# x + gamma * y on one core: from three row blocks with small lead loads to one block of 128 rows per partition, in fewer and larger transfers

## The chip, the core and the metric

The kernel runs on one core of one Trainium2 chip. The metric is device time in microseconds (us) of one execution. The core has compute engines that work side by side (here TensorE, called PE, and VectorE, called DVE, do the arithmetic), queues that only issue transfers in this kernel (SyncE, called SP, and ScalarE, called ACT), and 16 DMA engines that move data between HBM and the on-chip memory SBUF, which has 128 partitions.

## The reference

```python
B, S, D = 1024, 16, 512
x: bf16 (B, S, D)    y: bf16 (B, S, D)    gamma: bf16 (D)

def reference(x, y, gamma):
    return x + gamma * y
```

Seen as rows, x, y and the output are 16384 rows of 512 bf16 numbers, 1 KB a row. So 128 rows belong to each of the 128 partitions. x and y are 16.78 MB each and are read once; the output of 16.78 MB is written once: 50.33 MB in all, with very little arithmetic for it.

## The kernel before

**Layout.** The 16384 rows are cut into three blocks in HBM (`BLOCKS`, line 7): 4, 64 and 60 rows per partition. Inside a block, each partition owns consecutive rows, so partition p of the 64-row block starts 64 KB after partition p-1, and of the 60-row block 60 KB after it (`rows_of`). All of y stays in SBUF (`y_sb`, 128 rows per partition); x has a smaller buffer (`x_sb`, 76 rows), whose rows are used twice. The result is written over y in `y_sb` and stored from there.

**Transfers.** Two lists written out by hand give the order of the transfers. Below, y(4,68) means rows 4 to 67 of every partition. `SP` (lines 12 to 19) issues y(0,4), y(4,68), x(4,68), y(68,128), x(68,120), x(120,128). `ACT` (line 20) issues x(0,4), gamma, and the stores s(4,68), s(0,4), s(68,128). One issue cuts the transfer into one packet for each partition, as long as the partition's part (64 rows are 65536 bytes), so each of the 16 DMA engines gets 8 packets, and a 4-byte packet that signals a semaphore at the end. Each of the two issuing queues is worked off in the order of its issues.

**What holds an issue back.** The function `ring` (line 96) writes out both lists. `EARLY = (2, 1)` (line 22): the first two SP transfers and the first ACT transfer are put into the block of instructions that stands ahead of the start barriers of all engines. `HOLD` and `AHEAD` (line 24): the third transfer of SP and the second of ACT wait until PE has seen y(0,4) land (lines 149 to 151); DVE learns of that landing in the same way. x(68,120) is written into rows 24 to 75 of `x_sb`, so its issue waits for the add of piece 2; x(120,128) goes into rows 0 to 7 and waits for the add of piece 0. `RELEASE` (line 26): when x(68,120) has landed, PE lets ACT issue the stores (`s_go`, line 158) and lets DVE use the piece (`s_rel`, line 159). So no store is issued until nearly everything is loaded. A store also waits for the adds of the pieces that it holds.

**Arithmetic.** PE copies gamma to all partitions by a matmul with a row of ones (line 152), and DVE casts it to bf16 in SBUF (line 154). Then DVE works through its own list (line 28) over five pieces of 8, 16, 44, 52 and 8 rows: multiplications m0, m1, m2 (line 180), additions a2, a0, a1 (line 189), then m3, m4, a3, a4. Each is one instruction over a whole piece, in place in `y_sb`.

Of the kernel before, what the change touches and what calls it, by code (L numbers as in the profile page):

```python
# [3 lines left out]

BLOCKS = [4, 64, 60]

PIECES = [8, 16, 44, 52, 8]


SP = [
    ('y', 0, 4),
    ('y', 4, 68),
    ('x', 4, 68, 4),
    ('y', 68, 128),
    ('x', 68, 120, 24),
    ('x', 120, 128, 0),
]
ACT = [('x', 0, 4, 0), ('g',), ('s', 4, 68), ('s', 0, 4), ('s', 68, 128)]  # L20

EARLY = (2, 1)

HOLD, AHEAD = ('y', 0, 4), (2, 1)

RELEASE = ('x', 68, 120, 24)

DVE = [('m', 0), ('m', 1), ('m', 2), ('a', 2), ('a', 0), ('a', 1), ('m', 3), ('m', 4), ('a', 3), ('a', 4)]
MULT, ADD = mybir.AluOpType.mult, mybir.AluOpType.add
# [2 lines left out]
def _take(sem, n, eng):  # L32


    return eng.wait_ge(sem, n).then_inc(sem, -n)  # L35


def kernel(
# [9 lines left out]
    nc = tc.nc  # L48
# [8 lines left out]
    rows = N // P  # L57
    n = len(PIECES)
    assert sum(PIECES) == rows
    starts = [sum(PIECES[:c]) for c in range(n + 1)]  # L60
    dt = xf.dtype
    edges = [sum(BLOCKS[:c]) for c in range(len(BLOCKS) + 1)]
    assert edges[-1] == rows

    def rows_of(t, a, b):

        c = max(c for c in range(len(BLOCKS)) if edges[c] <= a)
        assert b <= edges[c + 1]
# [6 lines left out]
    y_sb = nc.alloc_sbuf_tensor("y_sb", [P, rows, D], dt).ap()  # L75
    x_loads = [w for w in ACT + SP if w[0] == "x"]
    y_loads = [w for w in SP + ACT if w[0] == "y"]
    stores = [w for w in SP + ACT if w[0] == "s"]
    for loads in (x_loads, y_loads, stores):
# [7 lines left out]
    s_load = {w: sem("s_" + "_".join(map(str, w[:2]))) for w in x_loads + y_loads}  # L87
    s_held = {nc.sync: sem("s_held_sp"), nc.scalar: sem("s_held_act"), nc.vector: sem("s_held_dve")}
# [4 lines left out]
    def meets(a, b, c, d):  # L93
        return a < d and c < b
# [4 lines left out]
    def x_at(row):  # L99
        return next(w[3] + row - w[1] for w in x_loads if w[1] <= row < w[2])  # L100
# [12 lines left out]
    def ring(eng, what, n_early, n_ahead):  # L113

        known, went = 0, False
        for k, w in enumerate(what):
            kind = w[0]
            if k == n_ahead:
                _take(s_held[eng], 1, eng)
            need = frees(w) if kind == "x" else pieces_of(w[1], w[2]) + list(w[3:]) if kind == "s" else []  # L120
            need = max((order[c] + 1 for c in need), default=0)
            if kind == "s" and not went:
                _take(s_go, 1, eng)
                went = True
            if need > known:
                eng.wait_ge(s_add, need)
                known = need
            if kind == "g":
                i = eng.dma_start(out=gamma_row, in_=gamma.unsqueeze(0)).then_inc(s_gamma, 16)
            elif kind == "x":  # L130
                to = x_sb[:, w[3] : w[3] + w[2] - w[1], :]
                i = eng.dma_start(out=to, in_=rows_of(xf, w[1], w[2])).then_inc(s_load[w], 16)
            elif kind == "y":
                r = slice(w[1], w[2])
                i = eng.dma_start(out=y_sb[:, r, :], in_=rows_of(yf, w[1], w[2])).then_inc(s_load[w], 16)
            else:
                r = slice(w[1], w[2])
                i = eng.dma_start(out=rows_of(of, w[1], w[2]), in_=y_sb[:, r, :]).then_inc(s_out, 16)
            if k < n_early:
                early.append(i.ins)  # L140

    ring(nc.sync, SP, EARLY[0], AHEAD[0])
    ring(nc.scalar, ACT, EARLY[1], AHEAD[1])


    nc.vector.memset(ones_row, 1.0).then_inc(s_ones, 1)  # L146
    _take(s_load[HOLD], 16, nc.tensor)
    for s_one in s_held.values():
        nc.tensor.sem_inc(s_one, 1)
    _take(s_ones, 1, nc.tensor)  # L150
    _take(s_gamma, 16, nc.tensor)
    nc.tensor.matmul(gamma_ps, ones_row, gamma_row, start=True, stop=True).then_inc(s_ps, 1)  # L152
# [3 lines left out]

    _take(s_load[RELEASE], 16, nc.tensor)
    nc.tensor.sem_inc(s_go, 1)
# [4 lines left out]
    def need(loads, c):  # L163
        for w in loads:
            if w not in landed and meets(starts[c], starts[c + 1], w[1], w[2]):
                if w == RELEASE:
                    _take(s_rel, 1, nc.vector)
                elif w == HOLD:
                    _take(s_held[nc.vector], 1, nc.vector)
                else:  # L170
                    _take(s_load[w], 16, nc.vector)
                landed.add(w)

    for kind, *args in DVE:
        c = args[0]
        yt = y_sb[:, starts[c] : starts[c + 1], :]
        if kind == "m":
            need(y_loads, c)
            g = gamma_sb[:, None, :].to_broadcast([P, PIECES[c], D])
            nc.vector.tensor_tensor(out=yt, in0=yt, in1=g, op=MULT).then_inc(s_dve, 1)  # L180
            open_mults += 1
        else:
# [4 lines left out]
            at = x_at(starts[c])  # L187
            xt = x_sb[:, at : at + PIECES[c], :]
            nc.vector.tensor_tensor(out=yt, in0=xt, in1=yt, op=ADD).then_inc(s_add, 1)  # L189
# [44 lines left out]
```

## Time and profile before

| | |
|---|---|
| median of 3 runs | 119.63 us (119.6 to 119.88) |
| span of the profiled execution, first to last instruction | 118.2 us |
| median less span (what lies around the span) | 1.4 us |
| DVE busy | 70.1 us, 59% of the span |
| PE busy | 0.6 us |
| bytes moved | 50.33 MB, 426 GB/s over the span |

The profile is one execution. Its times are in us from the span's start. It lists the compute instructions with their durations, the transfers with the moment of issue and of landing (a transfer has landed when its last semaphore signal arrives), and the DMA packets. For a window of time it gives the number of packets that start in it, their bytes, and their total time as a share of 16 engines over the window. So the mean time of one packet is share x 16 x window length / packets. A packet is counted with its full length in the window in which it starts, so a share over a short window can be over or under 100%.

The moments that the steps below use, from the timeline and the trace's landings (all us):

| transfer | issued | landed |
|---|---|---|
| y(0,4) | 0.00 | 3.38 |
| x(0,4) | 0.13 | 4.34 |
| y(4,68) | 0.42 | 23.81 |
| x(4,68) | 3.71 | 43.21 |
| gamma | 3.90 | 11.45 |
| y(68,128) | 4.09 | 61.34 |
| x(68,120) | 55.37 | 77.06 |
| x(120,128) | 57.58 | 79.53 |
| s(4,68) | 77.41 | 98.90 |
| s(0,4) | 77.81 | 100.12 |
| s(68,128) | 94.43 | 118.19 |

DVE's work: the memset of the ones 1.99, the cast of gamma 12.32, m0 to m2 from 23.95, a2, a0, a1 from 43.45, m3 and m4 from 61.80, a3 and a4 from 78.17 to 94.39.

### The profile page before, as it was taken

Reading aid. Unit: us, or ns where it says so; the run is one execution under the profiler, and the core shown is the slowest. Engines: PE = TensorE matmul, PEld = TensorE weight load, DVE = VectorE, ACT = ScalarE, POOL = GpSimd, SP = SyncE. Lnnn points to the kernel's source line nnn. Section 1 sums busy time; section 2 is a strip of 40 time slices with the busy share of each in tenths; the row PEclk is TensorE's granted clock in tenths of the full one; section 3 lists DMA queues with packets and bytes.
Section 4 is the critical chain, followed back from the end, with each engine's and each line's share of the span. In section 5 each row is a group of like instructions: output and inputs, shape, how many; then the busy total and the mean of one; then the engine's idle time right before and its main releaser. Section 6 shows DMA issues by size and latency. Waiting matters only on the chain. (4 is left out here: it accounts for less than half of the span.)

```text
span 118.2 us, 91 instructions
## 1 busy us (share of the span) xinstructions
PE 0.6 (0%) x1; PEld 0.1 (0%) x1; DVE 70.1 (59%) x12; POOL 0.2 (0%) x4
## 2 busy tenths in 40 slices
PE   0000100000000000000000000000000000000000
PEld 0000000000000000000000000000000000000000
DVE  0000200089999969999999999999999900000000
POOL 0000000000000000000000000000000000000000
DMA  6999889988899879879969696898899889799793
GB/s 248 461 666 399 355 355 399 665 355 355 355 599 466 355 333 624 374 333 499 499 288 576 288 576 288 360 637 355 355 576 488 355 355 510 333 582 416 333 499 166
DMA packets 1442, 50.33 MB, mean 426 GB/s; under 512 B 161, under 2 KB 162, under 8 KB 546
## 3 DMA queue, kind: packets, MB, share of 16 engines
q1 hardware_dynamic: 864, 33.03, 64.8%
q10 hardware_dynamic: 578, 17.30, 33.9%
HBM read 33.56 MB, written 16.78 MB: 426 GB/s over the span
## 5 line engine op out<-in xcount | busy, mean ns | idle before, releaser
L180 DVE TENSOR_TENSOR y_sb<-y_sb,gamma_sb 128x4096 bf16<-128x4096 bf16 (+3 forms) x5 | 34.7, 6981 | 10.9 <-DVEq L35 10.9
L189 DVE TENSOR_TENSOR y_sb<-x_sb,y_sb 128x4096 bf16<-128x4096 bf16 (+3 forms) x5 | 34.7, 6981 | 1.2 <-DVEq L35 1.1
L154 DVE CAST gamma_sb<-gamma_ps 128x512 bf16<-128x512 f32 x1 | 0.7, 692 | 10.2 <-DVEq L35 10.2
L146 DVE MEMSET ones_row<- 1x128 bf16 x1 | 0.2, 165 | 2.0 <-PEq L51 2.0
L152 PE MATMUL gamma_ps<-gamma_row,ones_row 1*128 1x512 bf16 x1 | 0.6, 581 | 11.6 <-PEq L35 11.6
L152 PEld LDWEIGHTS gamma_ps<-gamma_row,ones_row 1*128 1x128 bf16 x1 | 0.1, 101 | 11.6 <-issue 11.6
L218 POOL MEMSET const-bfloat16-1.0<- 128x1 bf16 x1 | 0.1, 101 | 0.0
L218 POOL MEMSET const-uint8-127<- 128x1 uint8 x1 | 0.1, 101 | 0.0
L218 POOL MEMSET const-float32-0.0<- 128x1 f32 x1 | 0.1, 98 | 0.2 <-issue 0.2
L218 POOL MEMSET const-float32-1.0<- 128x1 f32 x1 | 0.1, 98 | 0.0
## 6 DMA issues: line engine op xcount, KB each, us to landing
y_sb<-in_y_dram SPq DMA_DIRECT2D x1, 7680.0 KB, 57.3
out_dram<-y_sb ACTq DMA_DIRECT2D x1, 7680.0 KB, 23.8
x_sb<-in_x_dram SPq DMA_DIRECT2D x1, 6656.0 KB, 21.7
x_sb<-in_x_dram SPq DMA_DIRECT2D x1, 1024.0 KB, 22.0
y_sb<-in_y_dram SPq DMA_DIRECT2D x1, 512.0 KB, 3.4
x_sb<-in_x_dram ACTq DMA_DIRECT2D x1, 512.0 KB, 4.2
out_dram<-y_sb ACTq DMA_DIRECT2D x1, 512.0 KB, 22.3
y_sb<-in_y_dram SPq DMA_DIRECT2D x1, 23.4
```

The costliest lines, as they stand in the source:

```text
L146: nc.vector.memset(ones_row, 1.0).then_inc(s_ones, 1)
L152: nc.tensor.matmul(gamma_ps, ones_row, gamma_row, start=True, stop=True).then_inc(s_ps, 1)
L154: nc.vector.tensor_copy(out=gamma_sb, in_=gamma_ps).then_inc(s_dve, 1)
L180: nc.vector.tensor_tensor(out=yt, in0=yt, in1=g, op=MULT).then_inc(s_dve, 1)
L189: nc.vector.tensor_tensor(out=yt, in0=xt, in1=yt, op=ADD).then_inc(s_add, 1)
L218: nc = _bacc.Bacc("TRN2", target_bir_lowering=False, num_devices=1)
```

## The change

There is one block: partition p owns rows 128p to 128p+127, so its rows start 128 KB after those of partition p-1, in both loads and stores. y is loaded in two transfers of 64 rows, x in 64, 56 and 8, and the output is stored in two transfers of 64 rows. The pieces of DVE are 8, 12, 44, 56 and 8 rows, in the same order. Only y(0,64) stands ahead of the barriers. Nothing waits for a first landing any more: x(0,64), y(64,128) and gamma are issued as soon as the barriers are passed. x(64,120) goes into rows 20 to 75 of `x_sb` and waits for the add of piece 2 as before; x(120,128) goes into rows 0 to 7 and waits for the add of piece 0 as before. The stores wait for the landing of x(64,120).

```diff
-BLOCKS = [4, 64, 60]
+BLOCKS = [128]
-PIECES = [8, 16, 44, 52, 8]
+PIECES = [8, 12, 44, 56, 8]
 SP = [
-    ('y', 0, 4),
-    ('y', 4, 68),
-    ('x', 4, 68, 4),
-    ('y', 68, 128),
-    ('x', 68, 120, 24),
+    ('y', 0, 64),
+    ('x', 0, 64, 0),
+    ('y', 64, 128),
+    ('x', 64, 120, 20),
     ('x', 120, 128, 0),
 ]
-ACT = [('x', 0, 4, 0), ('g',), ('s', 4, 68), ('s', 0, 4), ('s', 68, 128)]
+ACT = [('g',), ('s', 0, 64), ('s', 64, 128)]
-EARLY = (2, 1)
+EARLY = (1, 0)
-HOLD, AHEAD = ('y', 0, 4), (2, 1)
+HOLD = None
+AHEAD = (None, None)
-RELEASE = ('x', 68, 120, 24)
+RELEASE = ('x', 64, 120, 20)
...
-    _take(s_load[HOLD], 16, nc.tensor)
-    for s_one in s_held.values():
-        nc.tensor.sem_inc(s_one, 1)
+    if HOLD:
+        _take(s_load[HOLD], 16, nc.tensor)
+        for s_one in s_held.values():
+            nc.tensor.sem_inc(s_one, 1)
```

## The prediction

> **What bounds the kernel now.** I read the DMA row of the 40 slices first, then the queues, then the chain of waits.
>
> ```profile
> span 118.2 us, 91 instructions
> ...
> DMA  6999889988899879879969696898899889799793
> ...
> q1 hardware_dynamic: 864, 33.03, 64.8%
> q10 hardware_dynamic: 578, 17.30, 33.9%
> ...
> issue 11%; DVE 3%
> ```
>
> The two queues' packets fill 64.8 + 33.9 = 98.7% of 16 engines' span, 116.7 us of 118.2. The trace's records of packets start at 1.00 and end at 117.85, so over the stretch in which there is anything to move the engines are full: the DMA engines are the bound, and DVE's 70.1 us are not. The low digits in the row are no gaps: a packet of 64 KB counts where it starts. The chain names little ("issue 11%") because it does not follow transfers. So the time is: 1.00 before the first packet, the packets of one DMA engine end to end, 0.36 until SP sees the last landing (117.85 to 118.21), and 1.4 around the span. The profiled span with 1.4 added is the median of the runs, 119.63; I make the sum against that.
>
> **What a packet costs.** Windows in which only one size starts give means (share x 16 x window / packets). In order: windows 82 to 97 (64 KB stores), 8 to 13 and 24 to 42 (64 KB loads), 101 to 117 (60 KB stores), 61 to 76 (52 KB loads), 98.6 to 99.2 (4 KB, its share includes rounding at the edges).
>
> ```profile
> q10 hardware_dynamic: 96, 6.29, 96.7%
> ```
> ```profile
> q1 hardware_dynamic: 32, 2.10, 97.1%
> ```
> ```profile
> q1 hardware_dynamic: 112, 7.34, 94.1%
> ```
> ```profile
> q10 hardware_dynamic: 112, 6.88, 99.2%
> ```
> ```profile
> q1 hardware_dynamic: 112, 5.96, 91.8%
> ```
> ```profile
> q10 hardware_dynamic: 63, 0.26, 104.3%
> ```
>
> This gives 0.967 x 16 x 15 / 96 = 2.418 us for a 64 KB store; for a 64 KB load 2.428 early and 2.420 later; 2.267 for 60 KB; 1.967 for 52 KB; 0.159 for 4 KB. The large ones all run at 27.1 bytes per ns. At that rate 4096 bytes would take 0.151, so each small packet wastes 0.008. No other operation of the kernel touches this sum.
>
> **Part by part, on one DMA engine** (8 packets for each transfer; group sums from the packet records, divided by 16 engines):
>
> - Removed: the three 4-row transfers, 24 packets of 4 KB. They took 1.36 (y) and 2.57 (x and store), 3.93 in all; at 0.159 they would be 3.82, so 0.11 is extra length of the very first packets.
> - Removed: 16 packets of 60 KB, 18.17 loaded and 18.14 stored, 36.31. Removed: 8 of 52 KB, 15.73.
> - Added: 16 packets of 64 KB, half loads, half stores: 16 x 2.419 = 38.70. Added: 8 packets of 56 KB. No row has this size; midway between 52 and 60 KB it is 2.117, bounds 1.967 and 2.267 for the price but hardly for the sum, as the bytes are fixed and the rate on both sides is 27.1; 8 x 2.117 = 16.93.
> - Removed: three transfers' semaphore packets on each engine, 9 ns each: 0.03.
>
> Sum: 38.70 + 16.93 - 3.93 - 36.31 - 15.73 - 0.03 = **-0.37**. If the 0.11 of the first packets returns on the first 64 KB ones, it is -0.26. The early 64 KB loads show that long packets get longer too (2.457 mean for the first 32, 2.428 for the next), so I keep most of it: **-0.28**.
>
> **The head.** y(0,4) is issued at 0.00 and its first packet starts at 1.00; y(0,64) is issued at the same place, as SP's first instruction. The other row for issue to first packet is the store of 64 KB packets, 77.41 to 78.73, 1.32, but on engines that were still busy with x(120,128). Ends: +0.32 (a long packet starts later) and -0.16 (the idle share between 1.0 and 2.0 goes, while the 16 engines start one after another). The nearest row is the load from SP with idle engines: 1.00, so nothing.
>
> **What the waits could spoil.** Each has cover, and I follow the landings to size it. The head is 8 rows shorter (2.54 in 4 KB packets, 2.65 with their extra), so y(0,64) lands near 21.2 and x(0,64) near 40.6. y(64,128) follows 8 x 2.42 later, 59.9; x(64,120) 76.8; x(120,128) 79.3; two stores of 19.34 each, 118.0.
>
> - The hold on y(0,4) goes: x(0,64), y(64,128) and gamma are issued near 2, not at 3.7 to 4.1. On SP nothing is gained, as y(0,64) fills the engines until about 20.4; this is also the cover, 18 us, for x(0,64) having to wait for the barriers. On ACT nothing stands ahead of gamma now but the barriers. It took 7.6 from issue to landing behind 64 KB packets; by that it lands before 11, PE and the cast add 1.6, and DVE first needs it at 21.2.
> - DVE: one row costs (14.02 - 11.89) / 8 = 0.267. m0 to m2 are 18.43 - 4 x 0.267 = 17.36, from 21.3 to 38.7; a2 starts at 40.8, and the three adds end at 58.1. m3 and m4 (16.22 + 4 x 0.267 = 17.29) start when y(64,128) lands, 60.0, and end at 77.3; a3 and a4 end at 94.9. DVE before was busy without a break from 43.45 to 94.39; now it has a rest of 1.9 before m3.
> - x(64,120) is issued at the end of a2, 52.8, x(120,128) at 55; the queue is not empty until 59.5. Cover 6.7 and 4.5; uncovered, each us late is a us.
> - The first store is let go at the landing of x(64,120), with x(120,128), 2.47 of packets, still to come: the same cover as before.
> - The last store is issued near 94.9, with 1.32 to its first packet 96.2; the first store keeps the engines busy until about 98.0. Before, it was 94.43 against 99.73. The cover falls from 4.0 to 1.8 but holds.
>
> So all of the change is -0.28: 119.63 - 0.28 = **119.35**. About 0.3% (0.36 us) is what a measurement of this kernel can tell from no change, so my likeliest case is "within 0.3%", on its fast side.
>
> **A rule against it.** Strided reading is in the trace: x(68,120) takes 52 of each 60 KB and its packets run at 27.08 bytes per ns, where stores without a stride reach 27.1. A pitch of 64 KB is there too, at 2.418. A pitch of 128 KB is not. The Trainium skill, "DMA: Bandwidth & Descriptors", section "Latency and other measured facts", says that copies between HBM tensors lose rate when the pitch from partition to partition in HBM is a large power of two: 207 GB/s at 512 KiB and 164 at 2 MiB, each way, against 214 when padded. It has no row for 128 KiB; if its loss at 512 KiB held here, an estimate from that page, the time would be about 3% longer, near 123. By the trace's rows, where 60 and 64 KB pitches run alike, the cost is nothing, and I go by those.
>
> **Rivals.**
>
> 1. *The start gets cheaper as well.* The first packets' extra (0.11 at 4 KB and 0.13 at 64 KB: 38.84 against 16 x 2.420 = 38.72) was due to small transfers from two queues meeting at 2.2 to 3.9, and the idle 0.16 goes. Then -0.37 - 0.13 = -0.50 to -0.66: 119.0 to 119.15. For it: the 64 KB loads of 3.65 start among the last packets of x(0,4). Against: packets that started at 13 to 18 are still long (97.4% x 16 x 5 / 32 = 2.435).
> 2. *A long first packet starts late*: +0.32 - 0.28, 119.67, no change.
> 3. *Slower: the 128 KB pitch.* 16 engines walk through HBM in step, 512 KB apart instead of 256 KB, and packets grow. Place: all 40 packets of 64 KB and 8 of 56 KB. Ends of the price: nothing, and what the worst row of 64 KB packets shows, the first 32 (2.457 against 2.418, +0.039): 48 x 0.039 = 1.87, so 119.35 + 1.87 = 121.2. It decides from (0.36 + 0.28) / 48 = 0.013 us per packet on. Against it: the same lengths at 60 and 64 KB pitch.
> 4. *DMA engines run dry before the last store*: only if DVE ends after 96.7, which would need 1.8 of new delay on it. I see none; small.
> 5. *It does not do what it says.* Were x(0,64) to go after the barriers only when y(0,64) has landed, the engines would stand still for about 1.5 near 20. No wait of that kind is in the SP list; negligible.
>
> **Numbers.** The case of 119.35, with 0.1 on both sides, has 0.5, and about a quarter of that lies beyond 0.3% faster. Rival 1 has 0.23, rival 2 has 0.09, rival 3 has 0.15, 4 and 5 have 0.03. Faster: 0.12 + 0.23 = 0.35. Slower: 0.15 + 0.03 = 0.18. Within: 0.47. The range is 118.95 to 119.95: it holds the likeliest case, rivals 1 and 2 with their bounds, and the mild part of rival 3.
>
> **What would show it.** Right: two queues' packets still fill the stretch from 1.0 to the end; 64 KB packets at 2.418 to 2.42 in windows of loads and of stores; 56 KB ones at 2.117; span near 117.9; last DVE add ending near 94.9, the last store's issue before the first one's packets end. Wrong: a first packet later than 1.3, 64 KB packets over 2.43 all along (rival 3), or a window late in the stores in which few packets run (rival 4). A span changed by more than 0.7 with packet lengths as before would mean that something outside the packet sum, which I take as fixed, has moved.

## The result, and the profile after

The changed kernel takes 120.05 us (median of 5, 119.88 to 120.24) against 119.65 of the kernel before, run beside it (119.6 to 119.88): ratio 1.0029, 95% interval [1.0018, 1.004]. It is slower by 0.3%, where 0.2% faster was forecast, and the time lies 0.1 us above the range that was forecast. The interval does not reach 1, so even less than the 0.3% that the prediction named can be told from no change.

The page of the changed kernel shows the same picture as before: the engines are full, in fewer packets.

```profile
span 118.6 us, 80 instructions
...
q1 hardware_dynamic: 720, 33.55, 66.1%
q10 hardware_dynamic: 290, 16.78, 32.7%
```

The two queues fill 98.8% of 16 engines' span, as they filled 98.7%, so there is still no gap to find. Either packets are longer than they should be, or the bytes are more, and the bytes are the same. So the length of the packets is read next, window by window: stores in 82 to 97, loads in 13 to 18, and then the second and the first packet of each engine (3.9 to 6.3, 1 to 2).

```profile
q10 hardware_dynamic: 96, 6.29, 96.7%
```
```profile
q1 hardware_dynamic: 32, 2.10, 96.7%
```
```profile
q1 hardware_dynamic: 16, 1.05, 100.8%
```
```profile
q1 hardware_dynamic: 16, 1.05, 311.8%
```

Stores take 0.967 x 16 x 15 / 96 = 2.418, loads 0.967 x 16 x 5 / 32 = 2.418, the second packet of each engine 1.008 x 2.4 = 2.419. But the first one takes 3.118 x 1 = **3.118 us**, 0.70 more. All 16 engines pay it side by side, once. The same window of the kernel before holds only 4 KB packets, which moved at 352 GB/s there (busy times of the engines, clock, DMA share, GB/s):

```profile
1.00:2.00 1.00, 0.00 (x0) 0.00 (x0) 0.01 (x1) 0.00 (x0) 1.00 0.94 352
```

DVE shows when the time was lost:

```profile
21.93 17.36 DVE L182 TENSOR_TENSOR y_sb<-y_sb,gamma_sb 128x4096 bf16<-128x4096 bf16 x3 [10.68 <-DVEq L36]
41.38 17.36 DVE L191 TENSOR_TENSOR y_sb<-x_sb,y_sb 128x22528 bf16<-128x22528 bf16 x3 [2.08 <-DVEq L36]
53.30 2.53 SPq L133 DMA_DIRECT2D x_sb<-in_x_dram  x2
60.62 17.29 DVE L182 TENSOR_TENSOR y_sb<-y_sb,gamma_sb 128x28672 bf16<-128x28672 bf16 x2 [1.88 <-DVEq L36]
77.80 17.96 ACTq L139 DMA_DIRECT2D out_dram<-y_sb  x2
78.09 17.30 DVE L191 TENSOR_TENSOR y_sb<-x_sb,y_sb 128x28672 bf16<-128x28672 bf16 x2 [0.18 <-DVEq L36]
```

The durations are those forecast (17.36 and 17.29), and every start is 0.5 to 0.65 late: 21.93 for 21.3, 41.38 for 40.8, 60.62 for 60.0. The shift is there at the first load and hardly grows. It happened before 21.

For each kernel I take the sum over its packets of what each lasts beyond the steady length of its size (2.418 for 64 KB, 2.267 for 60, 2.116 for 56, 1.966 for 52, 1.213 for 32, 0.607 for 16, 0.309 for 8, 0.159 for 4), divided by 16 engines. I call the part from packets that start in the first 5 us the **start loss**. The two profiled executions then differ like this:

| us, mean of 16 engines | before | changed | difference |
|---|---|---|---|
| start of the first packet | 1.12 | 1.14 | +0.02 |
| packets at steady length | 116.41 | 116.19 | -0.23 |
| start loss, and the same up to 20 us | 0.18, 0.25 | 0.70, 0.71 | +0.46 |
| extra length after 20 us | 0.06 | 0.12 | +0.06 |
| overlap of neighbouring records | -0.26 | -0.23 | +0.03 |
| mean end of the 16 engines | 117.59 | 117.93 | +0.35 |
| last engine behind the mean | 0.26 | 0.19 | -0.07 |
| last packet to end of span | 0.38 | 0.43 | +0.05 |
| span | 118.23 | 118.55 | +0.33 |

The gain in the packets came as forecast. In these two executions the start took twice as much; how much of that belongs to the kernels, the repeats r1 to r3 below show.

### The profile page after: what moved, and what is told of

Read it like the earlier page. It is cut to its first block, busy times and chain, and to the rows that moved or that the text cites. A ratio compares the mean times of both kernels' runs of the same rounds, so it can differ in the third digit from the quotient of the medians.

```text
span 118.6 us, 80 instructions
## 1 busy us (share of the span) xinstructions
PE 0.6 (0%) x1; PEld 0.1 (0%) x1; DVE 70.2 (59%) x12; POOL 0.2 (0%) x4
```

## The experiments

**Theory 1**: an engine that starts idle loses time once, and loses more when its first packet is long; small lead packets avoid part of it. **Rivals**: the pitch of 128 KB (theory 2); something the core does in the first microseconds, such as barriers and issues (theory 3). Later ones are named where they come up. The median of the kernel before moves between 119.65 and 119.81 with the chip, so kernels are compared by their ratio to the runs of it beside them.

**e1: a 4-row lead in the changed kernel.**

```diff
-    ('y', 0, 64),
+    ('y', 0, 4),
+    ('y', 4, 64),
-EARLY = (1, 0)
+EARLY = (2, 0)
```

> The changed kernel with one edit: y(0,64) is split into y(0,4) and y(4,64), both ahead of the barriers; the pitch stays 128 KB and nothing is held. Theory 1 (the first packet of an idle DMA engine is drawn out when it is long: 3.12 us on the mean in the changed kernel against 2.418 later): the first packets are 4 KB again, about 0.17 us, and the first 60 KB packets behind them are near 2.27 to 2.31; the 0.70 of the first round goes, and the time is near 119.4, some 0.6 below the changed kernel. Theory 2 (the 16 engines start in step on addresses 512 KB apart and hinder each other until they drift apart): 4 KB packets also start in step, so they are drawn out as well or the 60 KB ones behind them are, above 2.6; the time stays near 120.0. Theory 3 (whatever the core does up to about 4 us, barriers and the issues of x(0,64), y(64,128) and gamma at 1.4 to 2.3, takes from the engines): the 4 KB packets between 1.4 and 3 are drawn out too, in sum by 0.5 to 0.7 on each engine; time near 120.0.

119.73 us, ratio 1.0004 [0.9994, 1.0014]: the slowdown against the kernel before is gone, and the interval does not meet that of the changed kernel. The first 60 KB packets take 2.338 on the mean. The start loss falls from 0.70 to 0.45, not to the 0.18 of the first profile of before: the 4 KB packets had 0.38 extra. So theory 1 holds in its direction and at half its size, and a part of theory 3's expectation came too (small packets drawn out).

**e2: a pitch of 64 KB.** `BLOCKS = [64, 64]` in the changed kernel, nothing else.

> The changed kernel with two blocks of 64 rows, so that partitions stand 64 KB apart in HBM as before, and all else as in the changed kernel. Theory 1 (long first packet): the first 16 packets stay near 3.1 us, time near 120.0. Theory 2 (pitch): they fall to about 2.46, as the first 64 KB packets of the kernel before, time near 119.35. Theory 3 (the first 4 us of the core): they stay near 3.1, time near 120.0.

Ratio 1.0032 [1.0021, 1.0043], that of the changed kernel. The first 16 packets, in the window 1 to 2:

```profile
q1 hardware_dynamic: 16, 1.05, 301.6%
```

3.016 us: theory 2 falls.

**e9: pitches of 63 and 65 KB**, no power of two anywhere (theory 5). It came later, but belongs here.

```diff
-BLOCKS = [128]
+BLOCKS = [63, 65]
-    ('y', 0, 64),
-    ('x', 0, 64, 0),
-    ('y', 64, 128),
-    ('x', 64, 120, 20),
+    ('y', 0, 63),
+    ('x', 0, 63, 0),
+    ('y', 63, 128),
+    ('x', 63, 120, 20),
...
-PIECES = [8, 12, 44, 56, 8]
+PIECES = [8, 12, 43, 57, 8]
```

The stores are cut at row 63 as well, and `RELEASE` names x(63,120).

> The changed kernel with blocks of 63 and 65 rows instead of one of 128, so that partitions stand 63 KB and 65 KB apart in HBM and no distance between them is a power of two; y(0,63) alone stands ahead of the barriers and its packets are 63 KB; the 65-row transfers go out as two packets of 32.5 KB for each partition. Theory 1 (an idle engine that starts with a long packet loses 0.55 to 0.75 us, wherever it reads): the first packets are near 3.0 us, loss 0.6 to 0.7 in the first 5 us, time 120.05. Theory 5 (the engines read at equal offsets of power-of-two distances and hinder each other until they are spread in time by some 0.5 us): first packets near 2.45, loss under 0.2, time 119.4 to 119.6.

Ratio 1.0047 [1.0031, 1.0063]. Window 1 to 2:

```profile
q1 hardware_dynamic: 16, 1.03, 314.3%
```

3.143 us for 63 KB, whose steady length is 2.380: 0.76 too long. The pitch is not it.

**e3: y(0,64) behind the barriers.** `EARLY = (0, 0)`.

> The changed kernel with y(0,64) issued behind the barriers, like the other loads, so everything on the DMA engines starts about 1.1 to 1.5 us later. Theory 1: the first 16 packets are as long as in the changed kernel, about 3.1 us, and the time is that of the changed kernel plus the shift, 121.1 to 121.6. Theory 2: the same. Theory 3, where the barriers are the cause: they fall to about 2.46 and the time is only 0.5 to 0.9 above the changed kernel; where the issues that follow are the cause, nothing falls, and this run does not tell it.

121.42, ratio 1.0141 [1.0128, 1.0154]. The first packets start at 2.37 instead of 1.00 and last 3.179 (window 2.3 to 3.3, with gamma's two packets on the other queue):

```profile
q1 hardware_dynamic: 16, 1.05, 317.9%
q10 hardware_dynamic: 2, 0.00, 0.3%
```

The barriers are not it; whether the issues that follow play a part, this run does not tell. The load ahead of the barriers is worth 1.4 us (121.42 against 120.05).

**e4: first packets of 32 KB.** y(0,64) as y(0,32) and y(32,64), both early.

> The changed kernel with y(0,64) split into y(0,32) and y(32,64), both ahead of the barriers, so the first packets are 32 KB, which take 1.21 us at 27.1 bytes per ns. Theory 1 with an extra in proportion to the length (29%): first packets near 1.56 us, the next ones normal, time 0.35 below the changed kernel, 119.7. Theory 1 with a fixed extra for the first packet: near 1.9 us, time as the changed kernel, 120.05. Theory 3 (a stretch of time in which all is slow): first packets near 1.56 and the second ones, which start near 2.6, drawn out as well, together 0.70; time 120.05.

Ratio 1.0048 [1.0025, 1.0071]. First packets (window 1 to 2) and second ones (2.6 to 3.6):

```profile
q1 hardware_dynamic: 16, 0.52, 174.9%
```
```profile
q1 hardware_dynamic: 16, 0.52, 122.6%
```

1.749 and 1.226, against 1.213: 0.54 is lost in the first and 0.01 in the second. The loss is far from proportional to the length (0.35 would be), and nearly that of a 64 KB packet. This kernel's times spread widely (119.84 to 120.71). Its profiled execution, 120.67, has another 0.85 of long load packets after 45 us; that is not the start, and its cause is not known.

**e6: an engine that runs dry in the middle.** It was meant as "the kernel before without x(0,4) early":

```diff
-EARLY = (2, 1)
+EARLY = (2, 0)
-HOLD, AHEAD = ('y', 0, 4), (2, 1)
+HOLD, AHEAD = ('y', 0, 4), (2, 0)
```

> The kernel before with one edit: x(0,4) is not issued ahead of the barriers on ACT but held until y(0,4) has landed, so y(4,68) follows y(0,4) directly on SP's queue. It asks whether the second small transfer between the two is what keeps the loss at the start at 0.18 us on each engine. If it is (theory 1, the engines need some us of short packets): the loss is 0.40 or more and the time 119.9 to 120.1. If the contiguous y(0,4) does it alone (theory 4): 0.15 to 0.25, time 119.65.

It took 124.38, ratio 1.0386 [1.0371, 1.04], for a reason that I had not thought of: x(0,4) and gamma now stood on ACT's queue against 64 KB packets on SP's. An engine took a packet from each queue in turn, so the 8 small packets of x(0,4) on each engine went out between 7.4 and 23.6 (only the last two went together), and gamma behind them landed at 31.07, for 11.45 before. The window 7 to 24 holds as many packets of one queue as of the other:

```profile
q1 hardware_dynamic: 128, 7.34, 100.6%
q10 hardware_dynamic: 128, 0.52, 7.5%
```

DVE could not begin:

```profile
31.93 0.69 DVE L154 CAST gamma_sb<-gamma_ps 128x512 bf16<-128x512 f32 x1 [29.78 <-DVEq L35]
33.00 18.43 DVE L180 TENSOR_TENSOR y_sb<-y_sb,gamma_sb 128x4096 bf16<-128x4096 bf16 x3 [0.37 <-DVEq L35]
51.57 18.43 DVE L189 TENSOR_TENSOR y_sb<-x_sb,y_sb 128x22528 bf16<-128x22528 bf16 x3
63.49 2.53 SPq L132 DMA_DIRECT2D x_sb<-in_x_dram  x2
```

So x(68,120) was issued at 63.49, after the last y packet had ended at 61.29. That answers another question by accident: what a restart costs in the middle of the kernel, with the barriers and the first issues long past. Packets of 52 KB (steady 1.966) that start in 64 to 66, and the next ones in 66.9 to 68:

```profile
q1 hardware_dynamic: 16, 0.85, 129.6%
```
```profile
q1 hardware_dynamic: 16, 0.85, 178.8%
```

1.296 x 2 = 2.592, then 1.788 x 1.1 = 1.967: **0.63 lost on the mean of the 16 engines, once**. So the loss comes back where theory 3 has no place. For its own question the run tells little: its start loss is 0.38.

**e5: a lead that reads one stretch of 512 KB** (`BLOCKS = [4, 124]`, leads y(0,4), x(0,4), s(0,4), only y early), and **e7: the lead of e1 at a pitch of 64 KB** (`BLOCKS = [64, 64]`). Both try theory 4, that scattered first reads are slow.

> The kernel with the lead of e1, but the first 4 rows of each partition form a block of their own (4 and 124 rows), so the 128 packets of y(0,4) read one stretch of 512 KB instead of 128 places 128 KB apart; x and the store get a 4-row transfer too, none of them early. Packets of the first 5 us lost 0.18 us on each engine in the kernel before (contiguous lead), 0.45 in e1 (scattered lead), 0.70 in the changed kernel. Theory 1 (an engine that starts idle loses the same time wherever it reads): the loss is that of e1, 0.40 to 0.50. Theory 4 (the first reads from places that nothing has read yet answer late, and the loss grows with how scattered and how long they are): 0.15 to 0.25, as before. By packets alone it has 16 small packets more than e1 (0.13 us), so the time is near 119.85 by theory 1 and 119.6 by theory 4.

> The kernel of e1 with two blocks of 64 rows, so the 128 packets of y(0,4) are 64 KB apart instead of 128 KB, still scattered. Theory 1: loss in the first 5 us 0.40 to 0.50, time as e1, 119.7. Theory 4, if what counts is that the places are scattered at all: the same as e1. Theory 4, if it grows with the distance: between 0.18 and 0.45, time 119.5 to 119.65.

e5: ratio 1.0032 [1.002, 1.0043], start loss 0.40. Theory 4 falls (and r1 below lost 0.48 with the contiguous lead of the kernel before). e7: 1.0055 [1.0042, 1.0068], start loss 0.51 and another 0.32 by 20 us. Neither theory had expected that; a lead is not always enough. Part of e5's time is its end: the last engine finishes 0.46 behind the mean of the 16, in e1 0.24.

**e8: the kernel before without the hold.** `HOLD = None` and `AHEAD = (None, None)`.

> The kernel before with one part of the change alone: nothing waits for the landing of y(0,4), so x(4,68), y(68,128) and gamma are issued as soon as the barriers are passed, at about 1.9 to 2.7 us. Theories 1 and 4 both say that the hold costs and saves nothing: loss at the start 0.15 to 0.25, time 119.6 to 119.75. If the issues themselves hinder the engines in the first 4 us (what is left of theory 3): loss 0.40 or more, time 119.9 or more.

Ratio 1.0006 [0.9997, 1.0015]: the hold costs and saves nothing that can be seen. But the start loss was 0.43, though it begins with the transfers of the kernel before. So I profiled both kernels again, on one chip.

**r1, r2: the kernel before again; r3: the changed kernel again.**

> The kernel before once more, for a second profile. In its first profile the packets of the first 20 us lost 0.25 us on each engine; e8, which begins with the same transfers, lost 0.46. If the small start loss belongs to the kernel: 0.2 to 0.3 again. If that execution was a lucky one: 0.35 to 0.5.

> The kernel before, a third profile, with the same two expectations: a start loss of 0.2 to 0.3 on each engine if it belongs to the kernel, 0.35 to 0.5 if the first execution was a lucky one.

> The changed kernel once more, for a second profile. Theory 1: the first packets on the 16 engines are near 3.1 us again, loss of the first 5 us 0.6 to 0.8, and what its time has above 119.9 lies in loads after 45 us or in the spread of the engines.

r1 (119.83) and r2 (119.84): start loss 0.48 and 0.46. r3 (119.94): 0.67, first packets 3.088 (window 1 to 2):

```profile
q1 hardware_dynamic: 16, 1.05, 308.8%
```

So 0.18 was a low value: in the kernel before the loss varies with the execution, in the window 1 to 2 it moved 352 GB/s then and in r1 this:

```profile
1.00:2.00 1.00, 0.00 (x0) 0.00 (x0) 0.01 (x1) 0.00 (x0) 1.00 0.94 225
```

Against r2, r3 has -0.23 in the packets, +0.21 in the start loss, +0.08 because its engines' first packets start later (mean 1.20 against 1.12), +0.03 in overlaps: mean end +0.13, time +0.10. In this pair the new start just outweighs the gain.

**e10, e11: leads of one row and of sixteen rows** (y(0,1) and y(1,64); y(0,16) and y(16,64)), **e12: two queues** (y(0,32) on SP, y(32,64) on ACT behind gamma, all early).

> The kernel of e1 with a lead of one row instead of four: y(0,1) in packets of 1 KB, then y(1,64). Mean loss of the first round of packets on an engine so far: 0.70 and 0.67 us with 64 KB packets, 0.54 with 32 KB, 0.05 to 0.27 with 4 KB, where the second round loses another 0.01 to 0.18. Theory 1a (what is lost is the wait of a restarting engine, and short packets hide a part of it because several are under way at once): 1 KB packets run out after about 0.3 us, so the long ones behind them still meet the wait; loss in 5 us 0.5 to 0.7, time 119.85 to 120.0. Theory 1b (the first packet alone is slow, whatever follows): loss under 0.3, time 119.5.

> The kernel of e1 with a lead of sixteen rows: y(0,16) in packets of 16 KB, then y(16,64). Theory 1a: between the 4 KB and the 32 KB lead, loss in 5 us 0.45 to 0.55, time 119.75 to 119.85. Theory 1b (the first packet alone is slow, in proportion to its length): 16 KB take 0.61, a third more is 0.2; loss 0.2, time 119.5.

> The changed kernel with y(0,64) cut in two halves that start at once on the two queues, y(0,32) on SP and, behind gamma, y(32,64) on ACT, all ahead of the barriers; so each engine soon has two packets of 32 KB from two queues. e4 has the same two transfers one after the other on SP. Theory 1a (the wait of one packet is hidden by another under way): loss well below the 0.55 of e4, 0.2 to 0.4, though packets of two queues on one engine may be counted while they wait for each other; then the landing of both halves tells it: 21.2 instead of 21.5. Theory 6 (all 16 engines start at once and what they ask of together is not there faster): the loss stays 0.55 to 0.7, landing 21.5; time 119.9 to 120.1.

e10: ratio 1.0058 [1.0039, 1.0076]. The 1 KB packets are hardly drawn out (0.052 for 0.046), but run out between 1.4 and 1.8; the 63 KB packets behind them start at 1.5 to 2.5, 1.79 on the mean, and take 2.958 for 2.380; the start loss is 0.69. So it is not "the first packet" that is slow: the large packets behind the small ones pay (1a, not 1b). e11: 1.0009 [1.0, 1.0018], loss 0.57. e12: 1.0007 [0.9999, 1.0016], loss 0.62, but it did not try what it was meant to: ACT's half was issued at 0.68 and its first packet came at 5.19, so the first packets had no company. The loss is the one that theory 6 expected (0.55 to 0.7); the landing cannot be compared, as the second half came so late. In both the last engine ends only 0.17 behind the mean.

**e13, e14: the start of the kernel before in the changed kernel**, without and with the hold.

```diff
-    ('y', 0, 64),
+    ('y', 0, 4),
+    ('y', 8, 64),
-ACT = [('g',), ('s', 0, 64), ('s', 64, 128)]
+ACT = [('y', 4, 8), ('g',), ('s', 0, 64), ('s', 64, 128)]
-EARLY = (1, 0)
+EARLY = (2, 1)
```

> The changed kernel with the start of the kernel before: y(0,4) on SP and y(4,8) on ACT as small leads ahead of the barriers, y(8,64) behind the first; one block, two stores and no hold. If the start loss (0.67 to 0.70 us on each engine in the changed kernel) falls with two small leads to that of the kernel before (0.18 to 0.48), the packets alone give 116.31 against 116.41 there and 116.19 in the changed kernel: time 119.55 to 119.7, below both kernels or equal to the one before. If the lead is not what the kernel before owes its start to: loss 0.5 or more, time 119.85 or more.

> The kernel of e13 with the hold of the kernel before: x(0,64), y(64,128) and gamma wait for the landing of y(0,4). The kernel before without the hold took 1.0006 of its time, within the interval of no difference. If the hold is worth nothing: as e13 within 0.1. If it makes the small loss of 0.18 more frequent: 0.05 to 0.2 below e13.

Ratios 1.0012 [1.0002, 1.0021] and 1.0015 [1.0005, 1.0025], start loss 0.61 and 0.59 with 4 KB packets throughout. This speaks against a plain reading of theory 1: small leads lose less in most kernels, not in all.

| first packets | start loss (profiled executions) | ratio |
|---|---|---|
| 64 or 63 KB: changed kernel, r3, e2, e3, e9 | 0.70, 0.67, 0.60, 0.76, 0.76 | 1.0029, -, 1.0032, 1.0141, 1.0047 |
| 32 KB: e4, e12 | 0.55, 0.62 | 1.0048, 1.0007 |
| 16 KB: e11 | 0.57 | 1.0009 |
| 1 KB: e10 | 0.69 | 1.0058 |
| 4 KB: before, r1, r2, e8 | 0.18, 0.48, 0.46, 0.43 | (1) , -, -, 1.0006 |
| 4 KB: e1, e5, e6, e7, e13, e14 | 0.45, 0.40, 0.38, 0.51, 0.61, 0.59 | 1.0004, 1.0032, 1.0386, 1.0055, 1.0012, 1.0015 |

Each start loss is that of one execution, and the kernel before alone spans 0.18 to 0.48, so small differences between the rows mean little. Nor does the ratio follow the start loss: e5 and e7 lost 0.40 and 0.51 and have 1.0032 and 1.0055, e11 and e12 lost 0.57 and 0.62 and have 1.0009 and 1.0007.

The packet records show one thing more: the engines that start last lose least. Below are the first packets of e2 that start in 1 to 1.25 and in 1.25 to 2, then the packets of e6's restart that start in 64.4 to 64.7 and in 64.7 to 66.

```profile
q1 hardware_dynamic: 9, 0.59, 701.8%
```
```profile
q1 hardware_dynamic: 7, 0.46, 168.2%
```
```profile
q1 hardware_dynamic: 9, 0.48, 512.3%
```
```profile
q1 hardware_dynamic: 7, 0.37, 81.2%
```

In e2 that is 3.119 and 2.883 us, 0.70 and 0.47 too long; in e6 2.732 and 2.413, 0.77 and 0.45 too long. All nine executions whose first packets have 16 KB or more, or that restart with such packets, do the same: 0.64 to 0.92 for engines that start in the first quarter of a microsecond or so, 0.24 to 0.61 for the others. A price that each idle engine pays by itself, as in theory 1, would not depend on when it starts. It looks rather as if the engines share something that is slow at first (theory 6 in the expectation of e12); no run tested that by itself.

No version was faster than the kernel before; e1 and e12 cannot be told from it, with two transfers less and no hold.

## Why the prediction was wrong

**What bounds the kernel: right.** The engines are full from 1.00 to the end in both kernels, and the time follows their packets.

**The packet sum: right.** At steady lengths the changed kernel has 0.23 us less, where the terms without the 0.11 of the first packets gave 0.26. 64 KB packets are at 2.418 to 2.42 after the first round, and 56 KB ones at 2.116 (median) where 2.117 was interpolated.

**The head: wrong, and this is the step that failed.** It had two terms. The moment of the first packet, 1.00 from the row of the load with idle engines, was right: 1.002. Its length was the error: I let "the 0.11 of the first packets" return and kept most of it, -0.28 instead of -0.37, because the first 64 KB packets of the kernel before were only 0.039 too long. But those came at 3.65 behind 1 MB of small packets, on engines that were already running. A long packet on an idle engine had no row in that trace. It lost 0.70 (0.67 in r3), and what had been 0.25 up to 20 us became 0.71. A bound from both sides was due there: nothing, and, say, the share that the first sixteen 4 KB packets were too long (0.206 for 0.159, +30%), which for 64 KB is +0.72. That this comes out so near would be chance, as e4 showed that the loss is not proportional to the length. I gave a bound to the start of the first packet (+0.32) and none to its length.

**The profile it started from: a low one.** Of the +0.46 in the start loss about half is the low value of the first profile: against r2, r3 has +0.21. The time shows it too. In all the other profiled executions the time is 1.31 to 1.33 above the span (119.88 against 118.55 in the changed kernel), where the prediction took 1.4 from the median. So the first profile, with its span of 118.23, stands for an execution of about 119.55 (an estimate), faster than every timed run of the kernel before (119.59 at the least).

**The waits: right.** Every cover held. Gamma landed at 9.70, the last store was issued at 95.4 for 94.9, with the first store's packets running until 98.4 at least.

**The pitch: right**, for its lengths: after the first round the usual packet keeps its steady length at pitches of 128, 64 and 63 KB (median 2.418 in the changed kernel and 2.42 in e2 for loads of 64 KB, 2.380 in e9 for 63 KB). The long loads that e2's profiled execution has after 50 us stand in that of e4 too, at 128 KB. So the loss at 512 KiB that the prediction cites from the Trainium skill, "DMA: Bandwidth & Descriptors", section "Latency and other measured facts", has no counterpart here at 128 KB.

**The rivals.** Rival 1, a cheaper start, was the reverse of what came. Rival 2 had the right place, but a late packet instead of a long one, and ended at no change. Rival 3 had a long packet, but everywhere and by the pitch. None had a long first packet by itself.

**What is not settled.** The accounts explain the profiled executions, 119.88 and 119.94 of the changed kernel; its median of 120.05 lies higher, and the slower executions have no profile. On the mean, the two profiles of the changed kernel have 0.17 us more span than the three of the kernel before (start loss +0.31, packets -0.23), where the medians differ by 0.40; so more than half of the slowdown is seen in no profile. Why engines that start together lose time, and why the loss of 4 KB leads goes from 0.18 to 0.61, was not found; pitch, scatter, barriers and the hold made no difference that these runs show. What sets how far the last engine ends behind the mean (0.17 in e11 and e12, 0.46 to 0.51 in e5, e9 and e10) was not tried by itself, though it is a term of the sum that gives the span.

## What to carry to other kernels

In a kernel that the DMA engines bound, a start from idle engines had a price beyond the time to the first packet: 0.55 to 0.76 us with first packets of 16 to 64 KB, 0.18 to 0.61 with 4 KB, and 0.63 again in e6, where the engines ran dry in the middle. A packet's length is not to be taken from packets that started behind others when the one in question starts on an idle engine. Merging transfers saved some 0.008 us for each 4 KB packet that went, so look first at what the small transfers do for the start.

## What the runs showed of the hardware

- Transfers on two queues shared an engine packet by packet, not by bytes: 8 packets of 4 KB beside 64 KB packets took 16 us in e6, and the 1 KB of gamma behind them 27 us from issue to landing, against 1.3 us on an empty engine (e3: issued 1.39, landed 2.66).
- Load packets that start between about 50 and 58 us are a little long in most kernels (2.425 on the mean for 2.418 in the changed kernel), and 2.50 on the mean in the profiled executions of e2 and e4. Stores hardly ever are. No cause was found.
- Three transfers of 128 packets issued at 0.00, 0.13 and 0.42 in the kernel before had their first packets at 1.00, 2.21 and 3.65, as if their packets were made up one transfer after the other.
